# Retention followed by a two-layer ELU network: four chunk loads moved to later rounds, and 12 blank products in place of 25

## The chip, the cores and the metric

The kernel runs on one core of a Trainium2 chip. The metric is the time of one execution on the device, in microseconds (us); several executions are timed and their median is given. One execution was also taken with the hardware profiler; its views are what is quoted here. Engines go by these names: TensorE (PE in the profile, with PEld for its loads of stationary operands), VectorE (DVE), ScalarE (ACT), GpSimd (POOL) and SyncE (SP), which here issues the DMA transfers.

## What is computed

A retention recurrence over 768 steps, for 4 batches and 8 heads of width 64, followed by a two-layer network on the 3072 tokens that come out:

```python
gamma = 1.0 - 2.0 ** (-5.0 - np.arange(H))
for t in range(S):                                   # S = 768
    state = gamma * state + k[:, :, t] (outer) v[:, :, t]
    y[:, :, t] = scale * (q[:, :, t] @ state)
x = y.transpose(0, 2, 1, 3).reshape(3072, 512)
h = x @ w_in                                         # 512 x 2048
g = np.where(h > 0, h, np.exp(np.minimum(h, 0)) - 1) # ELU
return g @ w_out                                     # 2048 x 512
```

All arrays are fp32.

## The kernel before

**Tokens.** The recurrence is done in chunks of 128 tokens: 24 chunks, each 1 MB (128 x 2048, q and k, then v). `load()` (L113 to L125) takes one of four buffers of the pool "chunk" and issues the transfer on SyncE. A `retention_step` then makes scores (`sc`, L331), the running state (`kv`, L371) and outputs (`y`, L427, L442), after the values have been scaled by `scale_v` (L305, on GpSimd for all but the first chunks). Four chunks make a block of 512 tokens. Block 0 and block 1 are computed by themselves; blocks 2 to 5 are taken as two groups of 1024 tokens (`for nb in range(NB)`).

**The two matrix products.** They are done with Strassen-like schemes of fewer products, with sums of weights, inputs and outputs instead. In a group, the first GEMM begins with eight passes (`at` = 0 to 7) of the larger products at L1334. Then come eight rounds, n = 0 to 7, of products in fp32r (`passes`, L1397, and `big_rest`): the last part of the first GEMM. Each round makes two accumulators, `six` and `four`, of which each gets a third pass later; VectorE adds their parts (L957, L1903), ScalarE takes the two halves of the ELU's exponential (L1409, L1410), and VectorE ends the ELU (L1411), partly between tensors that both lie in SBUF. GpSimd meanwhile makes sums of the starting values (`seeds`, L1908 to L1912), and then sums of the ELU's outputs as the second GEMM needs them (L984). After the rounds comes the second GEMM (L1443), and within it the retention of the next group's first chunks.

**Weights** of the groups come from sums prepared earlier in DRAM (`scratch_dram`) through a ring of eight buffers, "wq", of 256 KB. `want()` lists the tiles in the order of use. `fetch()` (L893) issues the next one on SyncE as soon as a slot is listed as free; it is called by `done()`, which follows in the program the last product that reads a tile. On the chip the issue then waits on SyncE until TensorE has made that product. SyncE also issues the stores of prepared sums (L718) in the passes `at` of the first group, the chunk loads, and the stores of results. What stands behind a waiting issue waits too.

**The four chunk loads.** `more` is true only in the first of the two groups, so these loads, of chunks 16 to 19, exist once. Chunks 16 and 17 are issued in passes `at` = 5 and 6 (L2000, L2001), each after that pass's `side(at, 2)` and ahead of its stores. Chunks 18 and 19 are issued in rounds n = 2 and n = 5, after the round's last `passes` (L2056, L2057). Two of the four chunk buffers hold a part of the input (M1) from pass 2 on, which GpSimd reads for the last time at L1912; chunks 18 and 19 go there.

**The start.** Before the first chunk has landed, TensorE makes products of a tile `blank`: two rows of 128 x 512 (L1592), then a loop of 25 products of 64 x 64 (L1594 to L1599, recorded as L1596), into banks that are not read. An fp32 product of this kind is recorded as two matmul rows and two weight loads. Then `turn(0)` (L359) transposes a part of chunk 0.

Of the kernel before, what the change touches and what calls it, by code (L numbers as in the profile page):

```python
# [28 lines left out]
def kernel(  # L29
# [47 lines left out]
    CPB = TB // C  # L77
# [36 lines left out]
    def load(m, cuts=(0, 2048), behind=None):  # L114

        if m >= NCHUNK:
            return
        t = ldpool.tile([P, 2048], FP32, name="chunk", tag="chunk")
        raw[m] = (
            t[:, 0:1024].rearrange("p (a h c) -> p a h c", a=2, c=C),  # L120
            t[:, 1024:2048].rearrange("p (a h d) -> p a h d", a=2, d=D),
        )
        hold(t, behind)
        for lo, hi in itertools.pairwise(cuts):
            nc.sync.dma_start(t[:, lo:hi], qkv[m, :, lo:hi])  # L125

    def hold(t, other):

        if other is not None:
            nc.gpsimd.tensor_copy(t[0:1, 0:1], other[0:1, 0:1])  # L130
# [205 lines left out]
    def scores(tb, pp):  # L336

        sc = [ps_r.tile([P, 2, HP, D], FP32, name="sc", tag="r") for _ in range(2)]
        for x in range(2):
            score_products(sc, tb, pp, x)  # L340
        for a in range(2):
            nc.vector.tensor_tensor(
                out=raw[tb * CPB + 2 * pp + a][0][:, 1].rearrange("p h c -> p (h c)").rearrange("p (n t) -> p n t", t=D),
                in0=sc[a].rearrange("p x h t -> p (x h) t"),
                in1=cmask.unsqueeze(1).to_broadcast([P, 2 * HP, D]), op=ALU.mult,
            )
# [38 lines left out]
    def states(tb, pp):  # L385

        kvs = [ps_r.tile([P, 2, HP, D], FP32, name="kv", tag="r") for _ in range(2)]
        for x in range(2):
            state_products(kvs, tb, pp, x, range(2))
        for x in range(2):  # L390
            for sub in range(2):
                state_sum(kvs, tb, pp, x, sub)
# [323 lines left out]
    def send_small(count=None):  # L716
        for _ in range(min(count or len(to_send), len(to_send))):
            nc.sync.dma_start(*to_send.pop(0))  # L718
# [488 lines left out]
    def open_lifts():  # L1207
        if "left" in shared:
            shared["left"].close()
        shared["left"] = ctx.enter_context(ExitStack())  # L1210
        lifting.append(shared["left"].enter_context(tc.tile_pool(name="lifts", bufs=4, reuse_waits="tile")))
# [378 lines left out]
    def unread(count, n, to=warm):  # L1590
        for _ in range(count):
            nc.tensor.matmul(to[:, 0:n], lhsT=blank[:, 0:P], rhs=blank[:, 0:n], start=True, stop=True, skip_group_check=True)  # L1592

    unread(1, TB)  # L1594
    for n in range(25):
        nc.tensor.matmul(  # L1596
            (warm, other)[n % 2][rows(n // 2 % 2), 0:D], lhsT=blank[rows(n % 2), 0:D], rhs=blank[rows(n % 2), 0:D],
            start=True, stop=True, skip_group_check=True,
        )  # L1599
# [60 lines left out]
    def run(steps):  # L1660
        for _ in steps:
            pass
# [88 lines left out]
    def retention_step(tb, step):  # L1751
        if step == 0:
            scores(tb, 0)
            scores(tb, 1)
        elif step == 1:
            states(tb, 0)
            states(tb, 1)
        else:
            outputs_step(tb, step - 2)
# [94 lines left out]
    for s in sec:  # L1854
        if s == "first":
            step += 1
        at = (step, s if s in ("first", "middle") else "end")
# [24 lines left out]
    for nb in range(NB):  # L1882
        more = nb + 1 < NB
        q6, q4, u3, ends = {}, {}, {}, {}
        groups = 2 * nb + 4, 2 * nb + 5
# [16 lines left out]
        def c12_sum(m):  # L1902
            nc.vector.tensor_tensor(out=tile_of("C12", m), in0=q6[m], in1=tile_of("C12", m), op=ALU.add)  # L1903

        def seeds(*ms, first=False):
            places = [[tile_of(x, m) for x in ("C12", "C22", "M1")] for m in ms]
            for x, y, z in places if first else ():
                nc.gpsimd.tensor_tensor(out=z, in0=z, in1=y, op=ALU.add)  # L1908
            for x, y, z in places:
                nc.gpsimd.tensor_tensor(out=x, in0=x, in1=y, op=ALU.subtract)  # L1910
                if not first:
                    nc.gpsimd.tensor_tensor(out=y, in0=z, in1=y, op=ALU.add)  # L1912

        def begin(x, *ms):
            for m in ms:
                h = {"C21": q4, "C22": q6}.get(x)
                ends[x, m] = big_elu(x, m, h and h[m])
# [18 lines left out]
        def side(at, place):  # L1936

            if units and (at, place) in ((0, 2), (1, 2)):
                t = shared["x6"].tile([P, 2, 3, TH], F32R, name="wp", tag="x")
                made[:] = parts_of_layer(t, *units.pop(0), nc.vector)  # L1940
            elif made and place == 0:
                to_send.extend(made)
                made.clear()
                send_small()
            if nb == 0 and at in small_at and small_at[at][place]:
                j, n = small_at[at][place]
                some(smalls[j], n)
                if n == 3:
                    sent(j)
            if at in parts_of:  # L1950
                some(xparts, parts_of[at][place])
            for f, *args in c11_at.get((at, place), ()):
                f(*args)
# [12 lines left out]
        for at, (j, sub) in enumerate(ORDER1):  # L1966
            if at == 2:
                held_x = [ldpool.tile([P, 2048], FP32, name="chunk", tag="chunk") for _ in range(2)]
                G["M1"] = [x.rearrange("p (n f t c) -> p n f t c", n=2, f=2, t=2) for x in held_x]
            cur = big_twice(nb, j, sub)  # L1970
            next(cur)
            if at:
                next(tail, None)
            else:
                run(tail)
                open_lifts()
            side(at, 0)
            if at == 1 and nb == 0:
                retention_step(3, 2)
            next(cur)  # L1980
            if at < 7:
                run(tail)
            next(cur)
            side(at, 1)
            if nb == 0:
                if at == 0:
                    scores(3, 1)
                    states(3, 1)
            if at == 7:
                run(tail)  # L1990
                seeds(0, 1, first=True)
            next(cur)
            tail = cur
            if nb == 0:
                if at == 1:
                    retention_step(3, 3)
                    run(tail)
                    retention_step(3, 4)
            side(at, 2)
            if more and at in (5, 6):  # L2000
                load(groups[0] * CPB + at - 5)  # L2001
            if nb == 0 and at in stores:
                stores[at]()
                send_small()
# [8 lines left out]
        for n in range(2 * NQ):  # L2013

            passes(nb, n, 6, True, q6[n])
            if n > 1:
                c12_sum(n - 2)
            u3[n] = mpool.tile([P, 2, TH], FP32, name="m", tag="m")
            nc.scalar.copy(u3[n], q6[n])
            if n > 1:  # L2020
                begin("C22", n - 2)
            elif n == 0:
                begin("C11", 6)
            if n > 1:
                four(n)
            if n > 3:
                end("C12", n - 3)
            four_sum(n)
            if n < LAST:
                six(n + 1)  # L2030
            if n == 0:
                four(1)
            if n:
                begin("C21", n - 1)
                big_rest(nb, n - 1, q6[n - 1])
            if n < LAST:
                six_sum(n + 1)
            if n == 3:
                end("C12", 0)
            if n == 0:  # L2040
                end("C11", 2)
            elif n == 1:
                end("C21", 0)
                end("C11", 3)
                end("C11", 6)
            else:
                end("C22", n - 2)
                end("C21", n - 1)
            if n == 2:
                end("C11", 7)  # L2050
            if n > 1:
                begin("C12", n - 2)
            elif n == 1:
                begin("C11", 7)
            passes(nb, n, 4, True, q4[n])
            if more and n in (2, 5):  # L2056
                load(groups[0] * CPB + 2 + n // 5)  # L2057
            if n > 2:
                next(sec, None) if n < LAST else None
        big_rest(nb, LAST, q6[LAST])  # L2060
# [29 lines left out]
        for s in sec:  # L2090
# [5 lines left out]
            at = (step, s if s in ("first", "middle") else "end")  # L2096
            if more and at in VISITS:
                n = VISITS.index(at)
# [61 lines left out]
```

## Time and profile before

| what | us |
|---|---|
| median of three runs | 608.17 (607.33, 608.17, 608.63) |
| the profiled execution, its own time | 608.8 |
| its span (first to last instruction) | 607.0 |
| TensorE busy | 597.5 |
| VectorE busy | 511.4 |
| ScalarE busy | 261.6 |
| GpSimd busy | 96.2 |

The profile's first lines give the busy time of each engine, its share of the span and the number of instructions. The chain is the work that ended last, followed back from the end to what released each instruction; its shares tell which engine set the time. A row of waits reads: engine, output and line of the instruction that waited, what it waited for, microseconds in total, how many times, and the longest. A row of a timeline reads: start, length, engine, line, operation, output <- inputs, shapes, and the count of instructions joined in the row; in brackets the idle time ahead of it and what ended it. A row of windows reads: the stretch and its length, then busy time and instructions of PE, PEld, DVE, ACT and POOL, TensorE's granted clock, the DMA engines' busy share and GB/s. "L1397" is line 1397 of the kernel.

### The profile page before, as it was taken

How to read it: one execution, taken by the hardware profiler on the slowest of the kernel's cores; microseconds unless marked ns; L12 is line 12 of the kernel's file. 1: busy time of each engine (PE TensorE's matmuls, PEld its weight loads, DVE VectorE, ACT ScalarE, POOL GpSimd, SP SyncE). 2: the span in 40 equal slices, each digit the busy share in tenths (PEclk: the TensorE clock that was granted, in tenths of full speed). 3: DMA queues.
4: the chain of work that ended last, by engine and by line, in shares of the span. 5: the costliest groups of instructions: out<-in, count | busy, mean ns of one | idle time of the engine just before them, and what ended most of it. 6: DMA issues, size and time to landing. Idle time of an engine off the chain costs nothing.

```text
span 607.0 us, 13776 instructions
## 1 busy us (share of the span) xinstructions
PE 597.5 (98%) x5518; PEld 491.9 (81%) x5518; DVE 511.4 (84%) x779; ACT 261.6 (43%) x448; POOL 96.2 (16%) x77
## 2 busy tenths in 40 slices
PE   7899999999999999999999999999999999999998
PEld 5764668888889999888765888888888866788887
DVE  6768999989899987999899877898658999778885
ACT  5887945204553112247588310010136679611110
POOL 2010000000230100000797000020000299000000
PEclk9999999999999999999999999999999999999999
DMA  8789578879967998699976455784555576556553
GB/s 313 288 326 354 154 238 266 252 213 265 349 239 251 341 375 298 218 301 278 333 258 208 119 129 172 244 296 122 192 159 163 160 231 187 163 153 186 153 152 118
DMA packets 85824, 139.85 MB, mean 230 GB/s; under 512 B 6912, under 2 KB 46720, under 8 KB 81024
## 3 DMA queue, kind: packets, MB, share of 16 engines
q1 hardware_dynamic: 85760, 138.96, 71.1%
q8 instruction: 44, 0.72, 0.5%
q14 instruction: 20, 0.16, 0.1%
HBM read 105.12 MB, written 33.82 MB: 229 GB/s over the span
## 4 chain that ended last, share of the span: by engine, by line
PE 94%; DMA 2%; issue 1%; DVE 1%; ACT 0%; SPq 0%; DVEq 0%
PE pa L1443 16%; PE pa L1334 9%; PE pd L1443 8%; PE pa L823 5%; PE pd L1334 4%; PE pa L1017 4%; PE pb L1443 4%; PE x L1397 4%; PE pa L596 3%; PE x L686 3%; PE pb L1334 2%; PE pd L823 2%; PE pa L686 2%; PE pd L1017 2%; PE kv L371 2%; PE sc L331 2%
## 5 line engine op out<-in xcount | busy, mean ns | idle before, releaser
L1452 ACT COPY ms<-pa 128x256 f32<-128x256 f32 x41 | 15.2, 371 | 106.9 <-PE pa L1443 103.8
L1443 PE MATMUL pa<-gC,wq 128*128 128x256 f32 (+1 forms) x240 | 55.6, 377 | 0.0
L1443 PEld LDWEIGHTS pa<-gC,wq 128*128 128x128 f32 x240 | 44.9, 190 | 6.9 <-issue 1.0
L305 POOL TENSOR_TENSOR chunk<-chunk,vf 128x512 f32<-128x512 f32 x15 | 17.7, 1182 | 154.0 <-DMA chunk<-in_qkv_dram 150.3
L1410 ACT ACTIVATE r<-r 128x512 f32<-128x512 f32 x64 | 40.4, 631 | 2.0
L1456 DVE TENSOR_TENSOR res<-pd,ms 128x256 f32<-128x256 f32 x26 | 11.0, 422 | 27.8 <-PE pd L1443 17.0
L1345 ACT COPY m<-pa 128x512 f32<-128x512 f32 x32 | 18.7, 584 | 33.8 <-PE pa L1334 29.5
L1411 DVE SCALAR_TENSOR_TENSOR gC<-r,gC 128x512 f32<-128x512 f32 x24 | 29.7, 1244 | 0.0
L1443 PE MATMUL pd<-w_all,wq 128*128 128x256 f32 x120 | 28.4, 379 | 0.0
L965 POOL TENSOR_TENSOR wp<-wp 128x512 fp32r<-128x512 f32 x6 | 8.8, 1465 | 114.5 <-DMA scratch_dram<-wi 100.2
L183 ACT ACTIVATE w_all<-wraw 128x1024 uint32<-128x1024 uint32 (+1 forms) x19 | 19.1, 1008 | 16.7 <-PE x L686 9.6
L1908 POOL TENSOR_TENSOR chunk<-chunk,w_all 128x512 f32<-128x512 f32 x4 | 5.0, 1283 | 129.5 <-ACT w_all L1345 129.5
L1443 PEld LDWEIGHTS pd<-w_all,wq 128*128 128x128 f32 x120 | 22.8, 190 | 3.1
L1397 PE MATMUL x<-xl,wq 128*128 128x512 f32 x64 | 23.6, 454 | 0.8 <-DVE x L957 0.8
L1425 DVE TENSOR_TENSOR gC<-w_all,gC 128x1024 f32<-128x1024 f32 x20 | 24.2, 1260 | 0.0
L1443 PE MATMUL pa<-ts,wq 128*128 128x256 f32 x96 | 22.9, 381 | 0.0
L1443 PE MATMUL pa<-w_all,wq 128*128 128x256 f32 x96 | 22.9, 381 | 0.0
L185 ACT ACTIVATE w_all<-wraw 128x1024 fp8e4<-128x1024 f32 (+1 forms) x19 | 22.6, 1187 | 0.6
L1443 PE MATMUL pd<-ts,wq 128*128 128x256 f32 x96 | 22.7, 379 | 0.0
L213 DVE CUSTOM_DVE_ANT_0 w_all<-wraw,w_all 128x2048 uint16<-128x2048 uint16 (+1 forms) x19 | 20.7, 1089 | 1.2 <-DVE wraw L210 0.5
L596 PE MATMUL pa<-xb,w_all 128*128 128x512 f32 x48 | 21.5, 597 | 0.0
L1478 ACT COPY res<-pa 128x256 f32<-128x256 f32 x13 | 4.8, 372 | 38.1 <-PE pa L1443 38.1
(378 smaller groups left out, 1594.2 us busy)
## 6 DMA issues: line engine op xcount, KB each, us to landing
wq<-scratch_dram SPq DMA_DIRECT2D x231, 256.0 KB, 3.4
chunk<-in_qkv_dram SPq DMA_DIRECT2D x22, 1024.0 KB, 7.5
wraw<-in_w_dram SPq DMA_DIRECT2D x15, 1024.0 KB, 6.4
scratch_dram<-wp SPq DMA_DIRECT2D x8, 512.0 KB, 4.4
out_dram<-res SPq DMA_DIRECT2D x7, 512.0 KB, 3.0
scratch_dram<-gT SPq DMA_DIRECT2D x12, 256.0 KB, 4.0
wq<-scratch_dram SPq DMA_DIRECT2D x24, 128.0 KB, 3.3
scratch_dram<-w_all SPq DMA_DIRECT2D x12, 256.0 KB, 3.0
```

The costliest lines, as they stand in the source:

```text
L185: nc.scalar.activation(top, hi.bitcast(FP32), AF.Copy, scale=2.0**-120, saturate=False)
L213: vec.tensor_tensor(out=flat, in0=c, in1=flat, op=ALU.add)
L596: nc.tensor.matmul(hp, lhsT=w[n][:, fi, j // 2, j % 2, :], rhs=xb[:, j, :], start=(j == 0), stop=(j == 3))
L686: nc.tensor.matmul(X[j][:, d, :], lhsT=w[j][:, d * P : d * P + P], rhs=x[j], start=(n == 0 and d == 0), stop=at_end, skip_group_check=True,)
L823: nc.tensor.matmul(ps[:, fi, :], lhsT=w[:, fi, j2, :], rhs=x[:, j2, :], start=(begin and fi == 0 and j2 == 0), stop=(j2 == 1), skip_group_ ...
L1017: nc.tensor.matmul(ps, lhsT=w[:, f, :], rhs=ts[j][k][:, f, :], start=(begin and f == 0), stop=(f == 3), skip_group_check=True,)
L1334: nc.tensor.matmul(ps[:, f, :], lhsT=w[:, f, :], rhs=big_xs[j][k], start=(begin and f == 0), stop=True, skip_group_check=True,)
L1397: nc.tensor.matmul(joined(ps), lhsT=where[name][:, c : c + P].bitcast(F32R), rhs=x[:, k], start=(not third and c == 0), stop=(k == 1), ski ...
L1410: nc.scalar.activation(r, r, AF.Exp, scale=-1.0)
L1411: return lambda: nc.vector.scalar_tensor_tensor(g, r, -1.0, h, ALU.add, ALU.max)
L1425: nc.vector.tensor_tensor(out=quarter(to, r, t), in0=quarter(x, r, t), in1=quarter(y, r, t), op=op)
L1443: nc.tensor.matmul(ps, lhsT=w[:, f, :], rhs=ts[j][k][:, f // 2, f % 2, columns], start=(begin and f == 0), stop=(f == 3), skip_group_check ...
```

## The change

The loop of blank products runs 12 times instead of 25. The chunk loads leave the passes `at` = 5 and 6; the four loads of chunks 16 to 19 are now issued in rounds n = 0, 2, 4 and 6, each after the round's last `passes`. On SyncE these loads then stand behind 6, 5, 6 and 6 further tile issues of the ring. The order of work on VectorE, ScalarE and GpSimd is the same as before, and on TensorE it is the same but for the 13 blank products that are left out.

```diff
     unread(1, TB)
-    for n in range(25):
+    for n in range(12):
         nc.tensor.matmul(
             (warm, other)[n % 2][rows(n // 2 % 2), 0:D], lhsT=blank[rows(n % 2), 0:D], rhs=blank[rows(n % 2), 0:D],
             start=True, stop=True, skip_group_check=True,
@@
             side(at, 2)
-            if more and at in (5, 6):
-                load(groups[0] * CPB + at - 5)
             if nb == 0 and at in stores:
                 stores[at]()
                 send_small()
@@
             passes(nb, n, 4, True, q4[n])
-            if more and n in (2, 5):
-                load(groups[0] * CPB + 2 + n // 5)
+            if more and n % 2 == 0:
+                load(groups[0] * CPB + n // 2)
             if n > 2:
                 next(sec, None) if n < LAST else None
```

## The prediction

> **What bounds the kernel now.** I read the page first, then the waits of TensorE, then the chain that ended last around the changed lines, then the timeline of each engine beside the same stage of the second group of 1024 tokens, where no chunk is loaded.
>
> ```profile
> span 607.0 us, 13776 instructions
> PE 597.5 (98%) x5518; PEld 491.9 (81%) x5518; DVE 511.4 (84%) x779; ACT 261.6 (43%) x448; POOL 96.2 (16%) x77
> PE 94%; DMA 2%; issue 1%; DVE 1%; ACT 0%; SPq 0%; DVEq 0%
> ```
>
> TensorE is busy 98% of the span, and 94% of the chain is its own work. Only what it waits for, or what slows its products, can move the end; the change takes no product of the computation away. So the idle time of TensorE comes next, in order of size over the whole span:
>
> ```profile
> PE hp L572 <- issue: 1.6, 1, 1.6
> PE pa L1592 <- DVE blank L227: 1.4, 1, 1.4
> PE x L1397 <- DVE x L957: 0.8, 3, 0.4
> PE x L1397 <- DMA wq<-scratch_dram: 0.7, 1, 0.7
> PE pa L359 <- DMA chunk<-in_qkv_dram: 0.6, 1, 0.6
> ```
>
> The fourth row, one wait of 0.7 us for a weight tile of the ring, is the only one a moved chunk load can touch directly. The chain has it as "289.75 7.37 DMA wq<-scratch_dram": a tile issued at 289.75 landed at 297.1. SyncE's timeline shows what stood around it:
>
> ```profile
> 279.81 0.38 SPq L125 DMA_DIRECT2D chunk<-in_qkv_dram  x1
> ...
> 284.55 1.95 SPq L893 DMA_DIRECT2D wq<-scratch_dram  x3
> 288.98 0.33 SPq L125 DMA_DIRECT2D chunk<-in_qkv_dram  x1
> 289.75 2.05 SPq L893 DMA_DIRECT2D wq<-scratch_dram  x3
> ```
>
> Two chunks of 1 MB go out just ahead of these 256 KB tiles. In the trace they land 9.2 and 7.5 us after issue, the tiles between and behind them after 7.0 and 7.4 us. The page's median for a ring tile is 3.4 us; in the second group's same stage it is 3.0.
>
> **The moved loads.** TensorE in the two groups, the same products at the same point of the last part (group 0, then group 1):
>
> ```profile
> 295.33 1.09 PE L1397 MATMUL pb<-xr,wq 128*128 128x512 f32 x4
> 297.17 0.73 PE L1397 MATMUL x<-xr,wq 128*128 128x512 f32 x2 [0.75 <-DMA wq<-scratch_dram]
> ```
> ```profile
> 485.21 1.08 PE L1397 MATMUL pb<-xr,wq 128*128 128x512 f32 x4
> 486.12 0.61 PE L1397 MATMUL x<-xr,wq 128*128 128x512 f32 x2
> ```
>
> From the four products to the next two is 297.17−295.33 = 1.84 us in group 0 and 0.91 in group 1: 0.94 us lost (0.75 idle, and a row cut at the wait). Up to here both stages agree within 0.03 us. In the changed kernel the tile is still issued at 289.75 (its slot of the ring comes free only when TensorE reaches 289.73), but with no chunk in flight. With group 1's 3.0 us it lands at 292.8, with the page's 3.4 at 293.2, needed at 296.2. **−0.94 us**; zero only if something else holds the tile 6.5 us.
>
> The whole stage:
>
> ```profile
> 291.96:332.17 40.21, 38.65 (x135) 24.27 (x134) 36.76 (x48) 29.92 (x52) 37.22 (x24) 1.00 0.80 267
> 481.85:519.40 37.55, 37.55 (x135) 24.66 (x134) 35.28 (x49) 29.71 (x52) 32.59 (x20) 1.00 0.71 205
> ```
>
> The columns are length; busy time of TensorE, its weight loads, VectorE, ScalarE, GpSimd; clock; DMA share; GB/s. Both have 135 products at clock 1.00, yet group 0 is 2.66 us longer: 0.94 is the wait, 1.72 the rest. That rest comes from VectorE: in step with TensorE it ends each round, and in group 0 it is held twice by an ELU step of 128x512 that takes 0.67 us alone:
>
> ```profile
> 318.00 2.35 DVE L1411 SCALAR_TENSOR_TENSOR gC<-r,gC 128x512 f32<-128x512 f32 x1
> ...
> 323.27 2.24 DVE L1411 SCALAR_TENSOR_TENSOR gC<-r,gC 128x512 f32<-128x512 f32 x1
> ```
>
> Each lies beside a long GpSimd sum of L984 (317.41 for 2.39 us, 319.76 for 5.20). Group 1 has the same two steps at 506.43 and 510.49, at 1.15 and 2.23 us: one meeting and a graze. GpSimd's sums start on their own course, 0.62 us ahead of the stage in both groups; VectorE is the one shifted by the wait. Without the wait I let group 0 go group 1's course: **−1.72** (bounds: 0, if other phases bring the second meeting back; −1.72). I take the full value since without the wait the two stages have the same start.
>
> *The Trainium skill, "SBUF — State Buffer", section "Who interferes with whom", says that a VectorE instruction with two SBUF inputs and GpSimd exclude each other; the two rows (2.35 and 2.24 beside 0.67) agree. By that rule alone the length hangs on who comes first, so anything from 0 to −1.72 is possible, and by the page the sum lies between 606.3 and 608.0.*
>
> What the later loads cost: they are issued after rounds 0, 2, 4 and 6, which on group 1's course is about 297.7, 305.7, 314.9 and 324.4. SyncE then has 6, 5, 6 and 6 ring tiles between them. A chunk takes 0.33 to 0.38 us of SyncE and delays tiles behind it to some 7.4 us; those tiles are issued when a slot comes free, some eight tiles ahead of their use, and by the rows of group 1 that leaves 4 to 5 us of margin beyond a normal landing of 3.0. A tile behind a chunk takes 7.4−3.0 = 4.4 us of it: enough, by little. Cost 0 (bounds 0 to 0.9, one wait such as the old one). The two last chunks go to buffers that GpSimd's L1912 has read by 314.5; no wait there. The last chunk lands about 331; its scores run at 341, so 7 us are left or more.
>
> GpSimd scales the chunks' values (L305, 4 of about 1.2 us). Now at 324.91 to 330.0, with a wait for the last chunk; afterwards its first meets a VectorE step of L1411 near 325.7: **+0.38** (bounds 0 and one whole step, 1.04 us).
>
> **The blank products.** Thirteen fp32 products of 64x64 go, each two rows of matmul and two of weight load: 52 rows. In the timeline they run at 0.31 us and until 4.79 +0.33; then:
>
> ```profile
> 4.79 0.33 PE L1596 MATMUL pa<-blank 64*64 64x64 f32 x2
> 5.22 0.63 PE L359 MATMUL pa<-so,chunk 128*128 128x128 f32 x4
> ```
>
> The first real product waits for the first chunk (the 0.6 us row above), and the chain begins at "2.12 7.46 DMA chunk<-in_qkv_dram", the second chunk at 9.58. So removed blanks shorten nothing: **0**. They leave TensorE idle from about 4.2 to 5.2 us. What they do is keep it busy while its clock comes up: the first two blank rows of 128x512, at 1.45, take 2.08 us, where two of 128x256 at 14.33 take 0.70, so they start at half rate, and the narrow ones double about 3.3 us after that first product. Twelve still run to 4.2; whether the doubling is kept is R2 and R4 below.
>
> *The Trainium skill, "TensorE: Matmul & The Clock Gate", section "What's actually happening", speaks against this edit: the clock is half until an activity window of about 3.4 us was busy. The trace's 3.3 us agrees; an idle microsecond in a window may cost another window. By the page the time is then that of R2 or R4.*
>
> **The code.** The first row of the waits, 1.63 us "issue" at 27.96, comes after 5 of 8 products of L572. In the trace TensorE's code arrives in transfers of 16 KB, 44 for 11,036 rows, so some 251 rows each; the one it stands for was asked for at about 24.1, and TensorE goes on at 29.59, 5.48 us later, with the DMA engines 99% busy. 52 rows fewer put every boundary 52 rows later in the work: this wait goes (−1.63), but the two boundaries before it come to lie at about 20.6 and 24.5, 3.9 us apart where 5.48 are needed: a new wait of about 1.4 (0 to 1.7). **−0.2** (−1.6 to +0.1).
>
> **Sum**, on the profiled execution's own time of 608.8 (607.0 of span and 1.8 around it; 0.63 above the median 608.17 and 0.17 above the highest of the runs): −0.94 −1.72 +0.38 −0.2 + 0 = −2.48, so **606.3 us**.
>
> **Rivals.**
> R1: the meetings of VectorE and GpSimd come back in other places. For it: they are a matter of a few tenths of a microsecond. Against: group 1 shows a course with fewer. Then 608.8 −0.94 −0.2 and some 0.15 either way: about 607.5. Chance 0.14.
> R2: the clock rises one such window of 3.3 us later, near 8.4, so products between 5.2 and 8.4 run at half rate. The window 5.19 to 9.08 holds 3.34 us of TensorE work, most of it before the wait for the second chunk at 9.62, so some 0.5 to 1.5 us reach the path: 606.3+0.9 = 607.2. Chance 0.12.
> R3: the moved code boundaries make a stall elsewhere, where two bursts of short products lie close (128 in 2.0 us) and the DMA is loaded. The one of before cost 1.63; before shows only one in 44. About 606.3+1.5 = 607.8. Chance 0.10.
> R4, slower: the idle microsecond resets the clock, and half rate lasts until about 16.4. TensorE is busy almost without a break from 9.6 (5.09 of the 5.66 us between 9.62 and 15.28), so half of that time is lost: 0.5+(16.4−9.6)/2 = 3.9, or 606.3+3.9 = 610.2. It decides as slower from a rise later than about 15. For it: before, TensorE had no gap above 0.1 us between 1.45 and its wait at 9.0, so the trace shows nothing of a gap there. Against: twelve blanks and the wide product ahead keep it busy for about 2.7 us. Chance 0.14.
> Forecast 0.50.
>
> **How the numbers follow.** A measurement of this kernel can tell about 0.2% (1.2 us) from no change: faster is below 606.95, slower above 609.4. Faster: the forecast's 0.50, of which 0.03 is lost to its own spread, 0.03 of R1, 0.06 of R2 and 0.04 of R3: 0.60. Slower: R4's 0.14 and 0.02 for the bounds of the loads: 0.16. Same is what is left, 0.24: the other 0.11 of R1, 0.06 of R2, 0.06 of R3 and 0.01 of the forecast. The range goes from 605.2 (code wait gone whole, no port meeting: −3.6) to 609.0, which takes in R1, R2 and R3 and leaves out most of R4.
>
> **What would show it.** The wait of L1397 for a ring tile at 297 is gone; the tile issued near 289.75 lands before 294; the stage from 291.96 is near 37.9 us; VectorE's L1411 has one row above 2 us in it, not two. Near 28 us no "issue" wait, and one of 1 to 1.7 before. Products of L359 and L331 between 5.2 and 9 have the durations of before; if they double, R2 or R4 holds. I am wrong if a ring tile behind a moved chunk is waited for, or if the first 17 us grow.

## The result and the profile after

The changed kernel is slower: 610.29 us median (607.24 to 614.04, 22 executions) beside 607.37 (604.43 to 609.49, 22) for the kernel before, a ratio of 1.0060 with a 95% interval of 1.0043 to 1.0076. The profiled execution took 610.13 us, with a span of 608.4. The forecast of 606.3 and its range up to 609.0 are missed.

The waits of TensorE over the whole span of the changed kernel:

```profile
PE y L427 <- issue: 1.8, 1, 1.8
PE pa L1592 <- DVE blank L227: 1.5, 1, 1.5
PE pa L359 <- DMA chunk<-in_qkv_dram: 1.2, 1, 1.2
PE y L501 <- issue: 1.1, 1, 1.1
PE pd L442 <- DVE seen L459: 0.5, 2, 0.3
PE pa L572 <- DVE w_all L213: 0.5, 1, 0.5
```

The row for a ring tile of "wq" is gone. There are two "issue" rows where there was one. The row for a chunk is not the wait of before: that one, of 0.6 us, stood ahead of the second chunk's products,

```profile
9.62 0.66 PE L359 MATMUL pa<-so,chunk 128*128 128x128 f32 x4 [0.59 <-DMA chunk<-in_qkv_dram]
```

and this one, of 1.2 us, stands ahead of the first chunk's, as the timeline of the start shows below.

**The loads did what the forecast said.** The timeline of TensorE in the changed kernel, at the point where the wait had been:

```profile
299.21 1.07 PE L1397 MATMUL pb<-xr,wq 128*128 128x512 f32 x4
300.12 0.62 PE L1397 MATMUL x<-xr,wq 128*128 128x512 f32 x2
```

0.91 us from row to row, as in group 1, where before had 1.84. The tile lands 2.65 us after its issue instead of 7.37. VectorE's timeline in the same stage:

```profile
320.44 1.15 DVE L1411 SCALAR_TENSOR_TENSOR gC<-r,gC 128x512 f32<-128x512 f32 x1
...
324.51 2.25 DVE L1411 SCALAR_TENSOR_TENSOR gC<-r,gC 128x512 f32<-128x512 f32 x1
```

One meeting with GpSimd and a graze, 1.15 and 2.25 us; group 1 had 1.15 and 2.23, and before had 2.35 and 2.24 here. The whole stage, in the view by windows:

```profile
295.91:333.51 37.60, 37.60 (x134) 24.48 (x133) 35.15 (x49) 29.65 (x52) 36.01 (x23) 1.00 0.89 313
```

37.60 us beside 40.21. So 2.6 us were given back, against a term of −2.28 (−0.94 −1.72 +0.38). The +0.38 for the chunks' values does not show: group 1, which scales none there, took 37.55.

**The start is late.** TensorE's timeline at the first products:

```profile
5.53 1.09 PE L359 MATMUL pa<-so,chunk 128*128 128x128 f32 x4 [1.16 <-DMA chunk<-in_qkv_dram]
6.55 1.13 PE L331 MATMUL sc<-chunk 64*64 64x64 f32 x32
```

The rows of before read 0.63 and 0.70 for the same products: these run at about half rate. In the trace's record of the granted clock (the share of its full speed at which TensorE is let run) the full clock begins at 10.57 us instead of 4.90. By the first product of L572 (10.96 in before, 12.41 here) the loss is 1.45 us.

**The code waits moved.** Same view of the changed kernel, near 28 and 80 us:

```profile
25.47 0.69 PE L427 MATMUL y<-chunk 64*64 64x64 f32 x31
27.93 0.70 PE L427 MATMUL y<-chunk 64*64 64x64 f32 x33 [1.77 <-issue]
...
29.42 0.69 PE L442 MATMUL y<-chunk 64*64 64x64 f32 x32 [0.33 <-DVE seen L411]
```
```profile
78.82 0.40 PE L501 MATMUL y<-chunk 64*64 64x64 f32 x12
80.34 1.21 PE L501 MATMUL y<-chunk 64*64 64x64 f32 x60 [1.12 <-issue]
```

The first stands behind the 31st product of that burst of L427; it takes the place of before's 1.63 us in L572. The second has no counterpart before. That such waits are for code shows in where they fall: the profiles of this document, fourteen in all, hold 14 "issue" waits of TensorE above 0.1 us, and each comes at the same place, within a row, of a grid of 256 of TensorE's recorded rows (matmuls, weight loads and its sequencer's own). Its 11,280 such rows in before's trace arrive in 44 transfers of code, which makes 256 rows each. Laid beside before instruction by instruction, the changed kernel is 1.45 us behind at 11, 1.67 at 30, 2.91 at 77, 3.97 at 192 and, with the loads' gain, 1.36 at the end.

That accounts for the two profiled executions. But the medians are 2.9 us apart, not 1.4, so a part of the difference is not in this pair of traces.

### The profile page after: what moved, and what is told of

Its sections match the earlier page's. It is cut to its first block, busy times and chain, and to the rows that moved or that the text cites. A ratio compares the mean times of both kernels' runs of the same rounds, so it can differ in the third digit from the quotient of the medians.

```text
span 608.4 us, 13726 instructions
## 1 busy us (share of the span) xinstructions
PE 598.2 (98%) x5492; PEld 492.7 (81%) x5492; DVE 508.9 (84%) x779; ACT 261.9 (43%) x448; POOL 98.4 (16%) x77
## 4 chain that ended last, share of the span: by engine, by line
PE 77%; DVE 0%; issue 0%
PE pa L1443 16%; PE pa L1334 9%; PE pd L1443 8%; PE pa L823 5%; PE pd L1334 5%; PE pa L1017 4%; PE x L1397 4%; PE pb L1443 4%; PE pd L823 2%; PE pb L1334 2%; PE pa L1384 2%; PE pd L1017 2%; PE pa L1397 2%; PE sc L331 1%; PE y L483 1%; PE kv L371 1%
## 5 line engine op out<-in xcount | busy, mean ns | idle before, releaser
L305 POOL TENSOR_TENSOR chunk<-chunk,vf 128x512 f32<-128x512 f32 x15 | 19.9, 1332 | 147.7 <-DMA chunk<-in_qkv_dram 132.1
L1411 DVE SCALAR_TENSOR_TENSOR gC<-r,gC 128x512 f32<-128x512 f32 x24 | 27.8, 1167 | 0.0
```

The lines of the kernel that those rows point to most:

```text
L305: eng.tensor_tensor(out=v, in0=v, in1=vf[:, i].unsqueeze(2).to_broadcast([C, H, D]), op=ALU.mult)
L1411: return lambda: nc.vector.scalar_tensor_tensor(g, r, -1.0, h, ALU.add, ALU.max)
```

## The experiments

Theory A: the moved loads gain; leaving out blank products costs more, through a late clock and through code boundaries that now ask for their block at a worse moment. Rivals: B, the late clock alone; C, the loads themselves. All kernels take the changed kernel's code but for the edit shown, unless it says the kernel before. They are called e1 to e12 for short; "after" is the changed kernel's first profile, and e5 and e9 (the kernel before) and e8 (the changed kernel) are further profiles.

### The two edits apart

`e1_loads_only`, to which `e10_loads_again` is identical:
```diff
-    for n in range(12):
+    for n in range(25):
```


> The loads in rounds 0, 2, 4, 6 as changed, with all 25 blank products. Theory A (read from the two traces: TensorE's start at half clock costs 1.5 us, shifted code boundaries about 1.4, a VectorE meeting near 134 us 0.5, while the moved loads give 2.6 back): 2.6 us faster than before, ratio 0.9957, and a clock that doubles near 4.8 us. Theory B (the late clock alone is the loss, the rest is scatter of one execution): the same, 2.6 faster. Theory C (the moved loads themselves are what costs): 2 to 3 us slower, 1.004.

`e2_blanks_only`: the kernel before with
```diff
-    for n in range(25):
+    for n in range(12):
```


> Twelve blank products, the loads where they were. Theory A: 1.5 + 1.4 + 0.5 = 3.4 us slower and up to 5.5 if the medians' difference of 2.9 with 2.6 given back is taken instead; ratio 1.0056 to 1.009; products of 64x64 at half rate up to about 10.8 us. Theory B: 1.5 us slower, 1.0025. Theory C: within 0.2% of before.

Measured: e1 605.15 (604.68 to 607.05), ratio 0.9986 (0.9966 to 1.0006); e2 611.43 (607.58 to 613.27), ratio 1.0075 (1.0051 to 1.0100). C falls: the blanks alone make the loss, 0.75% or 4.5 us. The loads' gain has the right sign but is below the 2.6 us expected, and its interval still includes no gain at all. The waits of TensorE in e1 hold no code wait and no ring tile:

```profile
PE pa L1592 <- DVE blank L227: 1.5, 1, 1.5
PE pd L442 <- DVE seen L459: 0.5, 2, 0.3
PE y L442 <- DVE seen L411: 0.3, 1, 0.3
```

and those of e2 hold both kinds, a ring tile among them, since its loads are where they were:

```profile
PE y L501 <- issue: 1.4, 1, 1.4
PE pa L1397 <- DMA wq<-scratch_dram: 1.0, 1, 1.0
PE y L483 <- issue: 0.9, 2, 0.6
```

### Clock and code apart

`e3_twelve_wide` keeps TensorE busy to about 5 us with 12 products; `e4_blanks_split` leaves the idle time but brings the 13 products back later.
```diff
-            (warm, other)[n % 2][rows(n // 2 % 2), 0:D], lhsT=blank[rows(n % 2), 0:D], rhs=blank[rows(n % 2), 0:D],
+            (warm, other)[n % 2][rows(n // 2 % 2), 0:P], lhsT=blank[rows(n % 2), 0:D], rhs=blank[rows(n % 2), 0:P],
```


> As the changed kernel, but each of the 12 blank products is 128 columns wide instead of 64, so that TensorE is busy until about 4.8 us as before while its program has the changed kernel's 52 rows fewer. Theory A: clock back at 4.8 us, code waits near 28 and 80 us stay: 1.5 us less than the changed kernel, so 0.7 to 1.4 us slower than before by the medians, or 0.1 us faster by the traces. Theory B: the whole loss gone, 2.6 us faster than before, 0.9957. A rival on the clock (it rises at a moment that does not hang on the blanks but on the phase of a free-running window): the rise lies anywhere between 4.8 and 11 us here and in the other kernels.


```diff
     inner = plain_first()
+    for n in range(13):
+        nc.tensor.matmul(
+            warm[rows(n // 2 % 2), 0:D], lhsT=blank[rows(0), 0:D], rhs=blank[rows(0), 0:D],
+            start=True, stop=True, skip_group_check=True,
+        )
     next(inner)
```


> As the changed kernel, but the 13 blank products that were left out come back at about 12 us, ahead of the first product of L572, where TensorE waits 0.5 us for VectorE; so the idle time at 4.2 to 5.5 us stays, and the code boundaries from then on are those of before. Theory A: the late clock stays (1.5 us), the code wait near 80 us goes and the one near 28 us is that of before: 2.6 - 1.5 - 0.3 for the blanks that do not fit the gap = 0.8 us faster than before, 1.4 to 2.1 us faster than the changed kernel. Theory B: as the changed kernel, and 0.3 us slower.

Measured: e3 607.45 (606.82 to 609.81), ratio 1.0007 (0.9984 to 1.0030); e4 606.64 (605.52 to 611.24), ratio 1.0015 (0.9985 to 1.0046). Against e1's 0.9986 that is +0.21% (1.3 us) for the shifted code with the clock covered, and +0.29% (1.8 us) for the idle time with the code boundaries restored; each of these ratios has an interval of ±0.2% to ±0.3%. B falls with e3: covering the clock does not bring e1's time back. The times themselves, of the same rounds, say it more plainly: e1's twelve lie from 604.68 to 607.05, e3's from 606.82 up, 2.3 us apart in the median. e4 is less plain. Its times fall in two groups, seven from 605.5 to 606.9 and five from 609.2 to 611.2. The profiled one, 611.20, is of the upper group: its clock rises at 17.4 us, and it has before's code wait, "PE hp L572 <- issue: 1.7". What the clock did in the lower group no trace shows. e3's trace shows the second code wait and something behind it. Its timeline and its windows:

```profile
77.87 1.21 PE L501 MATMUL y<-chunk 64*64 64x64 f32 x60 [1.63 <-issue]
79.01 5.40 PE L596 MATMUL pa<-xb,w_all 128*128 128x512 f32 x8
```
```profile
77.87:79.42 1.55, 1.55 (x61) 1.36 (x61) 0.52 (x2) 0.00 (x0) 0.00 (x0) 1.00 0.92 159
79.42:82.83 3.41, 3.41 (x5) 1.35 (x4) 3.38 (x9) 0.00 (x0) 0.00 (x0) 0.50 0.88 327
82.83:86.00 3.17, 3.17 (x9) 1.36 (x8) 3.13 (x7) 1.23 (x2) 0.00 (x0) 1.00 0.03 7
```

The column ahead of the DMA share is the granted clock: 0.50 for 3.41 us right after the wait, 5 products in that time. Half of 3.41, 1.7 us, is lost on top of the 1.63. This is one execution: after and e8 have the wait and no such dip, and in e2, which has no record of the clock, the products behind the wait keep their rate (3.70 us for the eight that take 5.40 here). Of e3's twelve executions this alone has a mean granted clock below 1.000 (0.997), so the dip has no part in e3's median; four of the 34 executions of before in the same rounds have 0.997 too.

`e6_wide_split` has both edits at once, the wide blanks and the 13 later ones.

> Loads as changed, 12 blank products of 128 columns (TensorE busy to about 5 us), and 13 narrow ones at about 11 us, ahead of L572, so that from there on the code boundaries are those of the kernel before. Theory A (a code block asked for 0.7 us behind a 1 MB weight load near 73 us is queued behind it, one asked for 0.4 us behind is not): no issue wait in y L501, no clock dip behind it, 605.2 + 0.3 for the blanks that do not fit their gap = 605.5 us, about 2 us faster than the kernel with wide blanks alone. Rival (the wide blanks or the clock made the loss of that kernel): it stays at about 607.4.

Measured: 606.41 (605.24 to 610.18), ratio 0.9991 (0.9971 to 1.0010), profiled at 605.96. By the ratio it comes back to within 0.3 us of e1 and 1 us below e3; the intervals overlap, so the times alone do not tell it from the rival. The trace does: no issue wait at all, and the clock at 6.35 us. Its median is 606.4 where 605.5 was expected. Its highest time, 610.18, has a mean granted clock of 0.994 on record, and 0.6% of 608 us is 3.7 us, about what it lies above the median: the clock fell there too, at a place that no profile caught.

### How much idle time, how far a shift

`e7_18_blanks`:
```diff
-    for n in range(12):
+    for n in range(18):
```


> Loads as changed, 18 narrow blank products: idle time ahead of the first chunk about 0.4 to 0.8 us, code boundaries 28 rows later, so that the block near 73 us is asked for about 0.55 us behind the weight load. Theory A, if 0.4 us of idle time is enough to lose the clock's window: rise at 8.6 or later, 1 us lost, 606.2 without and 608 with the code wait. If it is not enough: rise between 4.9 and 8.3, 605.2 without and 607 with the code wait. Rival (the cost goes with the number of blank products left out): half way between 605.2 and 610.3, 607.7.

`e11_31_blanks`:
```diff
-    for n in range(12):
+    for n in range(31):
```


> Moved loads and 31 narrow blank products, busy to about 5.7 us at half rate; the code boundaries fall 24 rows earlier, so that the block near 70 us is asked for about 0.2 us behind the weight load. Theory A: clock rise between 4.9 and 8.3 us, no issue wait near 80 us; the first chunk's products up to 0.3 us later where the chunk lands early: 605.2 to 605.5. Rival (more blanks are better throughout): below 604.7. The earlier boundaries can bring a wait of their own near 23 to 27 us, where two lie 2.1 us apart: then 606.5.

Measured: e7 607.30 (605.18 to 610.45), ratio 1.0014 (0.9993 to 1.0035); e11 605.59 (605.13 to 606.42), ratio 0.9990 (0.9973 to 1.0006). e7's idle time is 4.79 to 5.31 us, its clock rises near 10.0, and it has no wait in L501: half a microsecond is enough to lose the clock. By the ratios e7 is 1.7 us above e1, but its trace gives only a part of that to the start: laid beside e1's it is 0.7 us behind at 16 us, and loses another 1.1 near 177 us, in products of L823 ("PE pd L823 <- DVE h L770: 0.7"). The expected 606.2 is a microsecond below the measured 607.30, which is near the rival's 607.7 on the count of blanks; the late clock in the trace speaks for theory A, the median alone does not. 31 blanks bring two short code waits (0.2 us at 11.9 and 0.3 at 27.2); they cost nothing that shows and gain nothing.

### The kernels again

> The kernel before once more, for a second profile. Theory A (the wait for a ring tile near 297 us and the two meetings of VectorE and GpSimd come from the loads): the wait and two L1411 rows above 2 us are there again, some 2.5 us. Rival (they were chance of one execution): they are gone. The code wait at the fifth product of L572 was there in one of two profiles with these code boundaries and 12 fewer microseconds of cover, and missing in another: 0 or 1.7 us; none near 80 us under either theory. Clock rise between 4.9 and 8.3 us.

> The changed kernel once more, for a second profile. Theory A: clock rise between 8.6 and 12.3 us, or one window later; an issue wait in y L501 near 80 us of 1.1 to 1.7 us again; no ring tile waited for near 297 us, one L1411 row above 2 us. Rival (both losses were chance of one execution): a rise before 8.3 us or no wait near 80 us.

> The kernel before, a third profile: it was 608.4 and 608.8 us in two profiled executions, where its timed ones lie between 604.1 and 611. Theory A (the loads' wait and the two meetings are there in every execution): again the wait of 0.6 to 0.7 us near 297 us and two L1411 rows above 2 us, whatever the time. Rival (a fast execution has neither): at a time below 606.5 us they are missing.

Measured, one execution each: e5 (before) 608.39 us, e8 (after) 611.39, e9 (before) 604.41. e5 repeats the loss of the loads, as its waits show:

```profile
PE x L1397 <- DVE x L957: 0.8, 3, 0.4
PE x L1397 <- DMA wq<-scratch_dram: 0.6, 1, 0.6
```

and two rows of L1411 at 2.36 and 2.24 us. e8 repeats the changed kernel: a late clock (14.95 us), again "PE y L501 <- issue: 1.0", and code waits of 0.6 in L427 and 0.5 in L483. In e9 the rival is right. The kernel before, with its loads where they always were, has no ring tile to wait for. SyncE's and TensorE's timelines in e9:

```profile
286.13 0.33 SPq L125 DMA_DIRECT2D chunk<-in_qkv_dram  x1
287.88 2.05 SPq L893 DMA_DIRECT2D wq<-scratch_dram  x3
```
```profile
293.46 1.08 PE L1397 MATMUL pb<-xr,wq 128*128 128x512 f32 x4
294.38 0.61 PE L1397 MATMUL x<-xr,wq 128*128 128x512 f32 x2
```

The second chunk goes out 1.75 us ahead of the tile (0.77 in the first profile), the tile lands after 6.04 us instead of 7.37, at 293.92, 0.46 ahead of its use, and VectorE's L1411 rows at 314.67 and 318.74 are 1.15 and 2.24 us, group 1's course. So the loss is a matter of half a microsecond: kept or lost whole, 2.6 us.

### The loads again

> All 25 blank products and the moved loads, timed once more. Theory A: 2.5 us faster than before (0.9959), no wait for a ring tile, one L1411 row above 2 us. Rival (the loads cost before only in some executions, as the first 12 runs allow): 0 to 1.5 us faster, with a smaller spread than before.

`e12_loads_012`, with 25 blanks:
```diff
-            if more and n % 2 == 0:
-                load(groups[0] * CPB + n // 2)
+            if more and n in (0, 1, 2, 5):
+                load(groups[0] * CPB + min(n, 3))
```


> All 25 blank products; chunks 16 and 17 are loaded in rounds 0 and 1, and 18 and 19 stay in rounds 2 and 5 as before. Theory A (only the two loads ahead of the last part cost, and a ring tile has 4 to 5 us to spare in the rounds): 2.5 us faster than before, as with rounds 0, 2, 4, 6. Rival (the spacing of the loads is what counts): three chunks in some 10 us delay a ring tile by more than it has to spare, a wait of 0.5 to 1 us for a tile between 300 and 312 us, and with it a second meeting of VectorE and GpSimd: 0 to 1 us faster than before.

Measured, beside 29 executions of before from 604.44 to 608.66 with a median of 605.69: e10 605.49 (604.65 to 605.88), ratio 0.9986 (0.9970 to 1.0001); e12 605.13 (604.10 to 606.52), ratio 0.9977 (0.9960 to 0.9993). For e10 the rival is right: a gain of 0.8 us, not 2.5, and a narrower spread. 11 of the 29 executions before lie above 607 us and none of e10's 12 lies above 605.9: the moved loads take the upper part of before's spread away and leave the rest as it was. 11/29 of 2.6 us is 1.0. Which of the 11 had the loss no trace tells. e12's rival falls: three chunks in succession, landing after 7.5 to 7.9 us each, delay no tile that is waited for, and the stage shows no ring tile in the waits. The loads that matter are the two ahead of the last part. e12 is the one version whose interval lies below before's time.

## Why the prediction was wrong

**The moved loads: the mechanism right, its weight wrong.** Every step came as written: the tile lands in 3 us, the 0.94 goes, VectorE takes group 1's course. In the traces −2.6 stands beside the −2.28 predicted. What failed is the step ahead of it, the sum "on the profiled execution's own time of 608.8": that execution was one of those that had the loss. In e9 the loss is absent, and by ratio the edit is worth 0.14% (0.8 us). The forecast priced a loss that hangs on a margin of 0.5 us as if it were in all executions.

**The blank products: "0" was the step that failed.** Leaving them out shortens nothing, as the prediction has it, but it was their work that brought the clock up in time. R2 and R4 named the mechanism, as side cases with 0.12 and 0.14. The rise of the clock in all profiles (the record of the granted clock, or the first short products at full rate):

| TensorE before the first chunk | full clock from (us) |
|---|---|
| busy: before, e5, e9, e1, e10, e12, e11, e3, e6 | 4.9, 7.4, 4.6, 6.2, 7.2, 6.4, 5.4, 7.7, 6.4 |
| idle 0.5 to 1.2 us: after, e8, e2, e7, e4 | 10.6, 15.0, 9.8, 10.0, 17.4 |

The two groups do not overlap. (e9 is idle from 4.99 to 5.50 us, after its rise.) R2's rise "near 8.4" came at 9.8 to 10.6, and its "0.5 to 1.5 us" was the right size for that (1.45 at 10.6 and 0.94 at 9.8, beside before's profile, one of the earliest to rise). A later rise costs more, as R4 had it: at the first product of L572 e8 is 1.6 us behind, at 16 us 2.7, and at L427 near 25 us 3.5, code wait included. What was wrong is the chance: a rise after 8.4 in five profiles of five. Two readings under that chance do not stand. The "0.6 us row" is the wait for the second chunk, at 9.62; ahead of the first, TensorE of before had no wait above 0.1 us, so it was the edit that opened the gap. And before has gaps of 0.13 us at 6.60 and 0.26 at 8.58, both after its rise, where the prediction saw none above 0.1.

*The Trainium skill, "TensorE: Matmul & The Clock Gate", section "What's actually happening", says that the window of 3413 ns runs freely and that the moment of the rise therefore varies by about 0.5 us. The stretch of 3.41 us at half clock in e3 agrees with the length; the rises of the busy group, from 4.6 to 7.7 us, vary by nearly a whole window instead. That rule does not explain why e8 and e4 rose later still, at 15.0 and 17.4: that stays open.*

**The code boundaries: place right, sum too small.** The swap near 28 us came as predicted in this pair of profiles, wait for wait (−1.63, +1.77); e8 and e2 have 0.6 there, e3 none. The second wait, R3's, was given 0.10 and is there in four of four profiles with 12 blanks and none put back later: after, e8, e2 and e3 (1.1, 1.0, 1.4, 1.6 us). The trace tells why. Near 70 us SyncE issues a 1 MB load of weights (`wraw`), and TensorE crosses a code boundary, in its products of L483, just behind it:

| kernel | boundary behind the load (us) | fetch of code begins behind the boundary | wait in L501 |
|---|---|---|---|
| e11 (31 blanks) | 0.19 | 0.69 | none |
| before, e5, e9, e1, e10, e12, e6, e4 | 0.36 to 0.37 | 0.5 to 1.5 | none |
| e7 (18) | 0.56 | 2.3 | none |
| after, e8, e2, e3 (12) | 0.72 to 0.73 | 4.6 to 5.1 | 1.0 to 1.6 |

The block is needed 5.5 us after it is asked for. 13 products of 64x64 fewer move the boundary by 0.36 us against the load, and the code then comes behind the load. That the fetch is queued behind the load is inferred from this order; no kernel took that load away. The earlier wait near 28 us, with its "−0.2", is more a matter of chance: with all 25 products in place ahead of it, it was there in before (1.63) and e4 (1.69) and missing in e5, e9, e1, e10, e12 and e6.

**The sum.** By ratios: late clock +0.28% (e7 against e1), code +0.21% (e3 against e1), loads −0.14%. The blanks together cost 0.74% (after against e1), 0.25% or 1.5 us more than these two; each ratio is uncertain by about 0.2%, so this remainder is neither shown nor excluded. By the medians of the same rounds the code alone is 2.3 us (e3 beside e1), which would leave little of it. Another candidate is in the traces: after, e2, e8 and e7, all with an idle start, lose 0.8 to 1.1 us in products of L823 between 134 and 180 us, e4 0.3, and none of the nine profiles with a busy start loses any there; e2 and e8 have code waits in L483 besides (0.9 and 0.5 us). Why L823 waits after a late start was not tested. The range has a slip of its own: its lower end, "−3.6", does not come out of its bounds, since −0.94 −1.72 −1.6 is −4.3, which gives 604.5 in place of 605.2. It has no part in the miss, which is at the other end.

**The scatter.** That 0.2% tells two kernels apart was true only of medians over many executions: single ones of before span 604.1 to 611.1.

## What to carry to other kernels

Work that seems to do nothing may hold a clock or a code boundary in place: before taking filler products away, ask which idle time opens and where every later boundary of the program falls against the large transfers. A loss that a profile shows must be asked how near its threshold lies: a tile that came 0.9 us late in one execution came 0.5 us early in another of the same kernel. Take a second profile of the kernel before, or the spread of its executions, ahead of pricing such a gain at its full size.

## What the runs showed of the hardware

An idle time of 0.5 us ahead of the first real product (e7) put the full clock off from 4.6 to 7.7 us to 10 us. A block of TensorE's code asked for 0.73 us behind a 1 MB load began its transfer 4.6 to 5.1 us later, one asked for 0.37 us behind it after 0.5 to 1.5 us. In one trace (e3) a wait of 1.63 us for code was followed by 3.41 us at half clock.
